# A gated GELU layer on one core: how the first 1024 rows of x and unit 0's weights are loaded, and the order of the opening

## The chip, the core and the metric

The kernel runs on one core of one Trainium2 chip. A core has five engines that run side by side: TensorE (PE) multiplies matrices, with a weight load (PEld) for each product; VectorE (DVE) and ScalarE (ACT) work elementwise and can read and write PSUM, the accumulators of PE; GpSimd (POOL) works elementwise on SBUF alone; SyncE (SP) only issues DMAs here. ScalarE can issue DMAs too. The core's 16 DMA engines serve all queues. The metric is the device time of one execution in microseconds, the median of several runs.

## The reference

```python
def reference(x, w_gate, w_up, w_down):
    g = jnp.einsum("bsd,df->bsf", x, w_gate)
    u = jnp.einsum("bsd,df->bsf", x, w_up)
    h = _gelu(g) * u                       # tanh form
    return jnp.einsum("bsf,fd->bsd", h, w_down)
```

x is 2048 rows of 1024, w_gate and w_up are 1024 x 3584, w_down is 3584 x 1024, all in bf16.

## The kernel before

The 2048 rows are done in two passes (`ip`) of two blocks of 512 rows each (`N = 512`; `c` is 0 or 1). For a product PE needs x with its model dimension on the partitions, so each block is held turned: `xT[c]` is a tile of 128 partitions x 8 x 512, eight slices of k (`NKB = 8`) of 128 each. The 3584 columns of the hidden layer are done in 14 units of 256 columns for gate and up each.

Unit 0 of the first pass is done plainly, in bf16: for each block 32 products of 128 x 128 by 512 (`plain`: eight slices of k for four banks of PSUM, gate and up for two halves of 128 columns), then `finish`: GELU on ACT (`gelu`, L212) and the product of gate and up on DVE (`times`). All later units save products by Strassen-like sums: seven products in place of eight, two of them raw (bf16, straight from x and w, `raw_products`, L227) and five in fp32r from sums that DVE makes of x (`t1` to `t4`, and the cast `tb` on ACT; `sums_t`, L169) and that DVE or POOL makes of the weights (`s1` to `s4`, and the cast `sa` on ACT; `sums_s`, L184). Sums of weights are made on DVE for unit 1 (its s3 on POOL), on POOL for the units after it; POOL is held behind the last t4 by a small copy (`pool_behind`, L199).

The opening, which the change touches, stands at L1038 to L1100:

- SP's queue: four plain loads of block 0's rows (`load_x`, 128 rows of 1024 each, 256 KB), six loads of unit 0's weights `wf` (gate and up in three pieces, k 0 to 1, 2 to 4, 5 to 7; 128, 192 and 192 KB each), unit 1's weights `w` (two loads of 512 KB), four transposing loads of block 1 (`transposing`, two slices of k each, 256 KB), unit 2's weights. A queue issues in this order. DMAs tell of their landing by eight semaphores used in turn, so an issue also waits for the landing of the one that had its semaphore before.
- PE: `NWARM = 7` products of ones into a bank that is overwritten later, then `turn` for each of the four loads of rows: eight transposes by the identity `ident`, which POOL makes, into a PSUM bank, and a copy to `xT[0]` by DVE (by ACT for the second). Two short products of ones stand ahead of the third `turn`. Then block 0's 32 products (the first two slices of k in halves of 256 rows), unit 1's 16 raw products, and, in `rest_of_0(0)` (L1093), block 1's 32 products into banks 4 to 7. Then unit 1's fp32r products: s2 by t2, s1 by t1, s3 by t3, s4 by tb (`unit`, L249), the raw products of units 2 and 3, and sa by t4.
- DVE, from the end of block 0: the two `times` of block 0 with one half of s1 each side of them, s2, s4, t1, t2, the sums of unit 1's raw products (`late`), half of t3, the `times` of block 1, the rest of t3, t4.

The order on SP, DVE, POOL and PE is that of the program; ACT's is too within the opening. Tiles come from pools in which a tile waits until the one that had its place has been read for the last time: the weights' pool has three places.

Of the kernel before, what the change touches and what calls it, by code (L numbers as in the profile page):

```python
# [7 lines left out]


@with_exitstack  # L10
def kernel(
# [23 lines left out]
    nc = tc.nc  # L35
    ENG = mybir.EngineType
    ORDER = {ENG.SP, ENG.DVE, ENG.Pool, ENG.PE}
    P = nc.NUM_PARTITIONS
    bf16 = mybir.dt.bfloat16
# [7 lines left out]
    x2 = x.flatten_outer_dims()  # L47
    out2 = out.flatten_outer_dims()
    S, Dm = x2.shape
    Df = w_gate.shape[1]  # L50

    NKB = Dm // P
    KH = NKB // 2
    NFB = Df // P
    NJ = NFB // 2
    N = 512
    NS = N // P
    NPASS = S // (2 * N)
    NU = NFB // 2
    NWARM = 7  # L60
    SLOTS, SUMS = 36, 13
    FIRST, LAST = 4, 13
    JS = {4: (0, 2), 6: (3, 5), 8: (6, 7), 10: (8, 9), 12: (10, None)}
# [20 lines left out]
    xpool = ctx.enter_context(tc.tile_pool(name="x", bufs=1))  # L84
# [8 lines left out]
    def new_x():  # L93
        return [xpool.tile([P, NKB, N], bf16, name=f"xT{c}") for c in range(2)]
# [11 lines left out]
    def h(kh, j, c):  # L106
        fb = kh * NJ + j
        return hT[:, fb, c, :] if fb < NH else late_h()[:, fb - NH, c, :]
    wdn = w_down.rearrange("(kh j p) d -> p kh j d", kh=2, p=P)

    def slot(shape, dtype, name, sums=False):
        return (spool if sums else kpool).tile(shape, dtype, name=name, tag="s" if sums else "k")
# [5 lines left out]
    bank = [psum.tile([P, N], f32, name=f"bank{i}") for i in range(8)]  # L118
    even, odd, cc, dd = bank[6:8], bank[0:2], bank[2:4], bank[4:6]

    def dve(out, a, b, op):
        nc.vector.tensor_tensor(out=out, in0=a, in1=b, op=op)  # L122
# [22 lines left out]
    def matmul(ps, lhs, rhs, start, stop):  # L145
        nc.tensor.matmul(  # L146
            ps, lhsT=lhs, rhs=rhs, start=start, stop=stop, skip_group_check=True
        )
# [3 lines left out]
    def load_w(u, queue=nc.sync):  # L152
        f0 = u * 2 * P
        w = wpool.tile([P, 2, NKB, 2 * P], bf16, name="w")
        for i, src in enumerate((w_gate, w_up)):
            queue.dma_start(
                out=w[:, i],
                in_=src[:, f0 : f0 + 2 * P].rearrange("(ko ki) f -> ki ko f", ki=P),
            )
        return w  # L160
# [8 lines left out]
    def sums_t(xT):  # L169
        K = range(KH)  # L170
        lo, hi = [[xT[c][:, k] for k in K] for c in range(2)], [
            [xT[c][:, KH + k] for k in K] for c in range(2)
        ]
        return Sums(
            how={
                "t1": lambda q: [new(dve, lo[1][k], lo[0][k], SUB, "t1") for k in K],
                "t2": lambda q: [new(dve, hi[1][k], q["t1"][k], SUB, "t2") for k in K],
                "t3": lambda q, K=K: [new(dve, hi[1][k], lo[1][k], SUB, "t3") for k in K],
                "t4": lambda q: [new(dve, hi[0][k], q["t2"][k], SUB, "t4") for k in K],
                "tb": lambda q: [cast(hi[1][k], "tb") for k in K],  # L180
            }
        )

    def sums_s(w, eng):  # L184
        GU = range(2)
        sh = [P, KH, P]
        a11, a21 = [[w[:, i, :KH, h : h + P] for i in GU] for h in (0, P)]
        a12, a22 = [[w[:, i, KH:, h : h + P] for i in GU] for h in (0, P)]
        return Sums(
            how={  # L190
                "s1": lambda q, GU=GU: [new(eng, a21[i], a22[i], ADD, "s1", sh) for i in GU],
                "s2": lambda q: [new(eng, q["s1"][i], a11[i], SUB, "s2", sh) for i in GU],
                "s3": lambda q: [new(eng, a11[i], a21[i], SUB, "s3", sh) for i in GU],
                "s4": lambda q: [new(eng, a12[i], q["s2"][i], SUB, "s4", sh) for i in GU],
                "sa": lambda q: [cast(a22[i], "sa", sh) for i in GU],
            }
        )
# [14 lines left out]
    def gelu(src):  # L212
        g = slot([P, N], f32, "g")
        nc.scalar.activation(g, src, ACT.Gelu_apprx_tanh)  # L214
        return g
# [3 lines left out]
    def times(fb, c, g, u):  # L219
        at = away[fb, c]() if (fb, c) in away else h(fb // NJ, fb % NJ, c)  # L220
        dve(at, g, u, MUL)
# [5 lines left out]
    def raw_products(e, c, xT, w):  # L227
        for i in range(2):
            product(e[i], w[:, i, :KH, :P], [xT[0][:, k, :] for k in range(KH)], True)
        p1 = [snap(e[i], "p1") for i in range(2)]  # L230
        for i in range(2):
            b21 = [xT[0][:, KH + k, :] for k in range(KH)]
            product(c[i], w[:, i, KH:, :P], b21, True)
        return p1
# [611 lines left out]
    sa = {}  # L846
# [152 lines left out]


    warm = nc.const_aps.tensor(1.0, [P, N], bf16)
    ident = xpool.tile([P, P], bf16, name="ident")
    make_identity(nc, ident)

    def load_x(c):
        t = []
        for i in range(NS):
            xn = slot([P, Dm], bf16, "xn")
            r0 = c * N + i * P
            nc.sync.dma_start(out=xn, in_=x2[r0 : r0 + P, :])  # L1010
            t.append(xn)
        return t

    def turn(xT, xn, c, i):
        tp = bank[4 + i].bitcast(bf16).rearrange("p (k r) -> p k r", k=NKB)
        for ko in range(NKB):
            nc.tensor.transpose(tp[:, ko, :], xn[i][:, ko * P : (ko + 1) * P], ident)
        for ks in (range(NKB),) if i < NS - 1 else (range(KH), range(KH, NKB)):
            ks = slice(ks.start, ks.stop)
            (on_act if i == 1 else on_dve)(out=xT[c][:, ks, i * P : (i + 1) * P], in_=tp[:, ks])  # L1020

    def transposing(xT, c, ko, r0, n=1):
        nc.sync.dma_start_transpose(
            out=xT[c][:, ko : ko + n], in_=x2[r0 : r0 + N, ko * P : (ko + n) * P]
        )

    def load_wf(queue, k0, k1):
        for i, src in enumerate((w_gate, w_up)):
            got = queue.dma_start(
                out=wf[:, i, k0:k1],  # L1030
                in_=src[k0 * P : k1 * P, 0 : 2 * P].rearrange(
                    "(ko ki) f -> ki ko f", ki=P
                ),
            )
            if queue is not nc.sync:
                tc.keep_in_program_order(got)

    xT = new_x()  # L1038
    xn0 = load_x(0)
    wf = wpool.tile([P, 2, NKB, 2 * P], bf16, name="w")  # L1040
    for k0, k1 in ((0, 2), (2, 5), (5, NKB)):
        load_wf(nc.sync, k0, k1)
    w = load_w(1)
    for ko in range(0, NKB, 2):
        transposing(xT, 1, ko, N, 2)
    ahead = load_w(2)

    def plain(ps, c, kos, parts=1):
        n = N // parts
        for k in range(kos.start, kos.stop, 2):  # L1050
            for part in range(parts):
                cols = slice(part * n, (part + 1) * n)
                for p, (j, i) in zip(ps, [(j, i) for j in range(2) for i in range(2)]):
                    for ko in (k, k + 1):
                        matmul(
                            p[:, cols],
                            wf[:, i, ko, j * P : (j + 1) * P],
                            xT[c][:, ko, cols],
                            ko == 0 and part == 0,
                            ko == NKB - 1,  # L1060
                        )

    def finish(ps, c):
        for j in range(2):
            times(j, c, gelu(ps[2 * j]), ps[2 * j + 1])

    on_dve, on_act = nc.vector.tensor_copy, nc.scalar.copy
    s, t = sums_s(w, dve), sums_t(xT)
    with tc.manual_schedule(engines={ENG.Activation}):
        def keep_warm(n, cols):  # L1070
            for _ in range(n):
                nc.tensor.matmul(
                    bank[3][:, :cols], lhsT=warm[:, :P], rhs=warm[:, :cols], start=True, stop=True
                )

        keep_warm(NWARM, N)
        for i in range(NS):
            if i == 2:
                keep_warm(2, 2 * P)
            turn(xT, xn0, 0, i)  # L1080
        plain(bank[0:4], 0, range(0, 2), parts=2)
        plain(bank[0:4], 0, range(2, NKB))
        s["s3"] = sums_s(w, pool)["how"]["s3"](s)
        s["s1"] = s["how"]["s1"](s, range(1))
        finish(bank[0:4], 0)
        s["s1"] += s["how"]["s1"](s, range(1, 2))
        nxt = {"p1": raw_products(odd, cc, xT, w)}
        s.make("sa", "s2", "s4")
        t.make("t1")

    seen = xpool.tile([P, 1], f32, name="seen")

    def rest_of_0(part):  # L1093
        if part == 0:
            plain(bank[4:8], 1, range(NKB))
            t.make("t2", "tb")
        else:
            t3 = t["how"]["t3"](t, range(0, 2))
            finish(bank[4:8], 1)
            t["t3"] = t3 + t["how"]["t3"](t, range(2, KH))  # L1100

    E, K, C, F = odd, cc, dd, even
    S, p5 = {}, {}
# [42 lines left out]
    for ip in range(NPASS):  # L1146
        with tc.manual_schedule(engines={ENG.Activation}):
# [10 lines left out]
            for u in range(1 if ip == 0 else 0, NU):  # L1158
# [113 lines left out]
                s = nxt.pop("s", None)  # L1272
# [35 lines left out]
        if not last:  # L1308
            t, s = got["t"], got["s"]
# [29 lines left out]
```

## Time and profile before

| what | value |
|---|---|
| median of 3 runs | 534.73 us (534.45 to 535.01) |
| the profiled execution | 534.41 us, of which the span of the instructions is 532.6 |
| busy: PE, DVE, ACT, POOL | 526.6, 404.7, 302.1, 268.4 us |
| HBM read, written | 86.38 MB, 31.06 MB |
| the four plain loads of block 0, issue to landing | 3.4 us in the median |
| the four transposing loads of block 1, issue to landing | 4.0 to 6.2 us |

A line of the timeline has the start, the time, the engine, the line, the operation, what it writes and reads, and the count, then the engine's idle time before it and what ended it. PE's products overlap, so a single one's time is longer than its share of the stream: a group's time divided by its count is the better measure. Most of the span is one unbroken stream of products:

```profile
371.51 21.38 PE bank L146 x95
392.89 0.07 issue
392.96 21.39 PE bank L146 x95
```

These lines are from the chain of work that ended last (start, time, what): 0.07 us lie between two stretches of 95 products.

### The profile page before, as it was taken

What the parts mean: (1) busy time and instruction counts of PE and PEld (TensorE: products, weight loads), DVE (VectorE), ACT (ScalarE), POOL (GpSimd) and SP (SyncE); (2) the same over time, 40 slices, a digit from 0 to 9 for tenths busy, and PEclk for the clock granted to TensorE, in tenths of its full rate; (3) what the DMA queues carried; (4) which work ended last, traced back from release to release, by engine and by line L of the source; (5) the groups of instructions that cost most, each with busy time, mean ns of one, the idle gap of its engine ahead of it and who ended that gap; (6) DMA issues with size and microseconds to landing.
All of it is one profiled execution on the core that took longest, in us unless ns stands there. A gap on an engine that the chain in (4) does not pass through costs nothing. (4 is left out here: it accounts for less than half of the span.)

```text
span 532.6 us, 7727 instructions
## 1 busy us (share of the span) xinstructions
PE 526.6 (99%) x2354; PEld 374.6 (70%) x2375; DVE 404.7 (76%) x646; ACT 302.1 (57%) x545; POOL 268.4 (50%) x259
## 2 busy tenths in 40 slices
PE   9999999999999999999999999999999999999997
PEld 5568686867677774588886676767668674588885
DVE  2988768787777786938799977576576679789795
ACT  2557686868585851015546866666656651064471
POOL 1179976979797970000002998695987900000000
PEclk9999999999999999999999999999999999999999
DMA  9966218585767599999899889954472399499994
GB/s 247 247 159 178 79 60 295 198 297 199 236 219 266 183 357 382 380 278 270 224 277 295 256 283 347 321 157 132 107 219 82 129 371 352 163 337 303 233 201 150
DMA packets 140601, 126.09 MB, mean 237 GB/s; under 512 B 31504, under 2 KB 119056, under 8 KB 140432
## 3 DMA queue, kind: packets, MB, share of 16 engines
q1 hardware_dynamic: 136208, 124.55, 77.4%
q10 hardware_dynamic: 4352, 1.05, 1.1%
q8 instruction: 19, 0.31, 0.2%
q14 instruction: 22, 0.18, 0.1%
HBM read 86.38 MB, written 31.06 MB: 221 GB/s over the span
## 5 line engine op out<-in xcount | busy, mean ns | idle before, releaser
L125 POOL TENSOR_TENSOR s<-w 128x512 fp32r<-128x512 bf16 x102 | 117.5, 1170 | 48.7 <-DMA w<-in_w_gate_dram 33.0
L146 PE MATMUL bank<-t,s 128*128 128x512 f32 x528 | 126.3, 392 | 0.0
L146 PEld LDWEIGHTS bank<-t,s 128*128 128x128 f32 x528 | 99.0, 188 | 21.6 <-POOL s L125 0.3
L146 PE MATMUL bank<-xT,w 128*128 128x512 bf16 (+1 forms) x489 | 107.8, 376 | 1.3 <-DMA w<-in_w_up_dram 0.3
L146 PEld LDWEIGHTS <-w 128*128 128x128 bf16 x504 | 47.9, 98 | 58.6 <-issue 3.9
L214 ACT ACTIVATE g<-sum 128x512 f32<-128x512 f32 x81 | 51.5, 636 | 59.4 <-DVE sum L122 58.6
L139 ACT COPY p<-bank 128x512 f32<-128x512 f32 x98 | 55.2, 590 | 46.5 <-PE bank L146 46.3
L122 DVE TENSOR_TENSOR hT<-g,bank 128x512 bf16<-128x512 f32 x72 | 49.0, 687 | 17.5 <-ACT g L214 11.3
L125 POOL TENSOR_TENSOR s<-w,s 128x512 fp32r<-128x512 bf16 x50 | 57.8, 1175 | 0.4
L125 POOL TENSOR_TENSOR s<-s,w 128x512 fp32r<-128x512 f32 x50 | 57.4, 1165 | 0.3
L146 PE MATMUL bank<-q 128*128 128x512 f32 x224 | 56.3, 391 | 0.0
L122 DVE TENSOR_TENSOR bank<-bank,p 128x512 f32<-128x512 f32 x74 | 51.3, 695 | 5.8 <-PE bank L146 5.3
L146 PE MATMUL bank<-t,sa 128*128 128x512 f32 x216 | 54.9, 397 | 0.0
L200 POOL COPY seen<-t 128x1 f32<-128x1 f32 x2 | 0.4, 183 | 107.4 <-DVE t L122 107.4
L146 PE MATMUL bank<-tb,s 128*128 128x512 f32 x216 | 54.3, 393 | 0.0
L146 PEld LDWEIGHTS bank<-q 128*128 128x128 f32 x224 | 42.0, 188 | 9.3 <-DMA q<-td 0.4
L146 PEld LDWEIGHTS bank<-t,sa 128*128 128x128 f32 x216 | 40.6, 188 | 9.1
L146 PEld LDWEIGHTS bank<-tb,s 128*128 128x128 f32 x216 | 40.5, 188 | 9.0 <-POOL s L125 0.3
L122 DVE TENSOR_TENSOR sum<-bank,p 128x512 f32<-128x512 f32 x54 | 37.0, 686 | 12.7 <-PE bank L146 11.3
L139 ACT COPY u<-bank 128x512 f32<-128x512 f32 x62 | 35.5, 596 | 17.7 <-PE bank L146 14.1
L134 ACT CAST tb<-raw 128x512 fp32r<-128x512 bf16 x20 | 11.9, 635 | 38.3 <-DMA raw<-in_w_down_dram 32.0
L134 ACT CAST sa<-w 128x512 fp32r<-128x512 bf16 x54 | 30.7, 617 | 3.7 <-DMA out_dram<-st 3.7
(123 smaller groups left out, 733.4 us busy)
## 6 DMA issues: line engine op xcount, KB each, us to landing
raw<-in_w_down_dram SPq DMA_DIRECT2D x72, 256.0 KB, 5.7
w<-in_w_gate_dram SPq DMA_DIRECT2D x27, 512.0 KB, 4.6
w<-in_w_up_dram SPq DMA_DIRECT2D x27, 512.0 KB, 6.2
td<-m SPq DMA_DIRECT2D x11, 768.0 KB, 5.1
q<-td SPq DMA_DIRECT2D x28, 256.0 KB, 5.5
pd<-xT SPq DMA_DIRECT2D x10, 512.0 KB, 5.8
w<-td SPq DMA_DIRECT2D x5, 1024.0 KB, 9.3
p<-pd SPq DMA_DIRECT2D x20, 256.0 KB, 5.1
```

What stands on the lines that cost most here:

```text
L122: nc.vector.tensor_tensor(out=out, in0=a, in1=b, op=op)
L125: nc.gpsimd.tensor_tensor(out=out, in0=a, in1=b, op=op)
L134: nc.scalar.copy(out=t, in_=src)
L139: nc.scalar.copy(out=t, in_=ps)
L146: nc.tensor.matmul(ps, lhsT=lhs, rhs=rhs, start=start, stop=stop, skip_group_check=True)
L200: nc.gpsimd.tensor_copy(out=seen, in_=tile[:, :1].bitcast(f32))
L214: nc.scalar.activation(g, src, ACT.Gelu_apprx_tanh)
```

## The change

Block 0 is no longer loaded as rows and turned on PE, but by four transposing loads on SP's queue, at its very start, as block 1 is; block 1's four follow at once, ahead of unit 1's weights. Unit 0's weights are issued on ScalarE's queue. The identity, the 32 transposes and the copies out of PSUM are gone, the two short products of ones too; there are eight long ones in place of seven. Block 0's products are no longer split by halves. Block 1's products stand right behind block 0's, ahead of unit 1's raw ones. On DVE the order is: the `times` of block 0, t1, t2, s1, s2, the `times` of block 1, half of t3, the sums of unit 1's raw products, the rest of t3, s4, t4. What comes behind is unchanged.

```diff
@@ -4,7 +4,6 @@
 import concourse.tile as tile
 from concourse import bass_utils, mybir
 from concourse._compat import with_exitstack
-from concourse.masks import make_identity
 
 
 @with_exitstack
@@ -57,7 +56,7 @@
     NS = N // P
     NPASS = S // (2 * N)
     NU = NFB // 2
-    NWARM = 7
+    NWARM = 8
     SLOTS, SUMS = 36, 13
     FIRST, LAST = 4, 13
     JS = {4: (0, 2), 6: (3, 5), 8: (6, 7), 10: (8, 9), 12: (10, None)}
@@ -999,25 +998,6 @@
 
 
     warm = nc.const_aps.tensor(1.0, [P, N], bf16)
-    ident = xpool.tile([P, P], bf16, name="ident")
-    make_identity(nc, ident)
-
-    def load_x(c):
-        t = []
-        for i in range(NS):
-            xn = slot([P, Dm], bf16, "xn")
-            r0 = c * N + i * P
-            nc.sync.dma_start(out=xn, in_=x2[r0 : r0 + P, :])
-            t.append(xn)
-        return t
-
-    def turn(xT, xn, c, i):
-        tp = bank[4 + i].bitcast(bf16).rearrange("p (k r) -> p k r", k=NKB)
-        for ko in range(NKB):
-            nc.tensor.transpose(tp[:, ko, :], xn[i][:, ko * P : (ko + 1) * P], ident)
-        for ks in (range(NKB),) if i < NS - 1 else (range(KH), range(KH, NKB)):
-            ks = slice(ks.start, ks.stop)
-            (on_act if i == 1 else on_dve)(out=xT[c][:, ks, i * P : (i + 1) * P], in_=tp[:, ks])
 
     def transposing(xT, c, ko, r0, n=1):
         nc.sync.dma_start_transpose(
@@ -1036,68 +1016,52 @@
                 tc.keep_in_program_order(got)
 
     xT = new_x()
-    xn0 = load_x(0)
     wf = wpool.tile([P, 2, NKB, 2 * P], bf16, name="w")
     for k0, k1 in ((0, 2), (2, 5), (5, NKB)):
-        load_wf(nc.sync, k0, k1)
-    w = load_w(1)
+        load_wf(nc.scalar, k0, k1)
+    for ko in range(0, NKB, 2):
+        transposing(xT, 0, ko, 0, 2)
     for ko in range(0, NKB, 2):
         transposing(xT, 1, ko, N, 2)
+    w = load_w(1)
     ahead = load_w(2)
 
-    def plain(ps, c, kos, parts=1):
-        n = N // parts
-        for k in range(kos.start, kos.stop, 2):
-            for part in range(parts):
-                cols = slice(part * n, (part + 1) * n)
-                for p, (j, i) in zip(ps, [(j, i) for j in range(2) for i in range(2)]):
-                    for ko in (k, k + 1):
-                        matmul(
-                            p[:, cols],
-                            wf[:, i, ko, j * P : (j + 1) * P],
-                            xT[c][:, ko, cols],
-                            ko == 0 and part == 0,
-                            ko == NKB - 1,
-                        )
+    def plain(ps, c):
+        for k in range(0, NKB, 2):
+            for p, (j, i) in zip(ps, [(j, i) for j in range(2) for i in range(2)]):
+                for ko in (k, k + 1):
+                    matmul(
+                        p, wf[:, i, ko, j * P : (j + 1) * P], xT[c][:, ko],
+                        ko == 0, ko == NKB - 1,
+                    )
 
     def finish(ps, c):
+        g = [gelu(ps[2 * j]) for j in range(2)]
         for j in range(2):
-            times(j, c, gelu(ps[2 * j]), ps[2 * j + 1])
-
-    on_dve, on_act = nc.vector.tensor_copy, nc.scalar.copy
+            times(j, c, g[j], ps[2 * j + 1])
+
     s, t = sums_s(w, dve), sums_t(xT)
     with tc.manual_schedule(engines={ENG.Activation}):
-        def keep_warm(n, cols):
-            for _ in range(n):
-                nc.tensor.matmul(
-                    bank[3][:, :cols], lhsT=warm[:, :P], rhs=warm[:, :cols], start=True, stop=True
-                )
-
-        keep_warm(NWARM, N)
-        for i in range(NS):
-            if i == 2:
-                keep_warm(2, 2 * P)
-            turn(xT, xn0, 0, i)
-        plain(bank[0:4], 0, range(0, 2), parts=2)
-        plain(bank[0:4], 0, range(2, NKB))
+        for _ in range(NWARM):
+            matmul(bank[3], warm[:, :P], warm, True, True)
+        plain(bank[0:4], 0)
+        finish(bank[0:4], 0)
+        t.make("t1")
+        plain(bank[4:8], 1)
+        t.make("t2", "tb")
         s["s3"] = sums_s(w, pool)["how"]["s3"](s)
-        s["s1"] = s["how"]["s1"](s, range(1))
-        finish(bank[0:4], 0)
-        s["s1"] += s["how"]["s1"](s, range(1, 2))
+        s.make("sa", "s1", "s2")
+        finish(bank[4:8], 1)
         nxt = {"p1": raw_products(odd, cc, xT, w)}
-        s.make("sa", "s2", "s4")
-        t.make("t1")
 
     seen = xpool.tile([P, 1], f32, name="seen")
 
     def rest_of_0(part):
         if part == 0:
-            plain(bank[4:8], 1, range(NKB))
-            t.make("t2", "tb")
+            t["t3"] = t["how"]["t3"](t, range(0, 2))
         else:
-            t3 = t["how"]["t3"](t, range(0, 2))
-            finish(bank[4:8], 1)
-            t["t3"] = t3 + t["how"]["t3"](t, range(2, KH))
+            t["t3"] += t["how"]["t3"](t, range(2, KH))
+            s.make("s4")
 
     E, K, C, F = odd, cc, dd, even
     S, p5 = {}, {}
```

## The prediction

> **What bounds the kernel now.** I read the page first, then PE's waits, then the first 25 us in order of time, then the DMA queues.
>
> ```profile
> span 532.6 us, 7727 instructions
> PE 526.6 (99%) x2354; PEld 374.6 (70%) x2375; DVE 404.7 (76%) x646; ACT 302.1 (57%) x545; POOL 268.4 (50%) x259
> PE bank L1072 <- PEq L1323: 0.8, 1, 0.8
> PE bank L146 <- DMA w<-in_w_up_dram: 0.3, 1, 0.3
> ```
>
> The last two lines are all that PE waits for in the whole span: 0.8 us for the start, 0.3 us for one piece of unit 0's weights. PE is the bound throughout; what the opening saves or loses on PE goes into the total one for one, unless a later wait takes it back.
>
> ```profile
> 0.77 3.14 PE L1072 MATMUL bank<-const-bfloat16-1.0 128*128 128x512 bf16 x7 [0.77 <-PEq L1323]
> 3.71 1.91 PE L1017 MATMUL bank<-ident,xn 128*128 128x128 bf16 x16
> 5.42 0.44 PE L1072 MATMUL bank<-const-bfloat16-1.0 128*128 128x256 bf16 x2
> 5.70 1.08 PE L1017 MATMUL bank<-ident,xn 128*128 128x128 bf16 x16
> 6.72 0.38 PE L146 MATMUL bank<-xT,w 128*128 128x256 bf16 x2
> 9.83 7.50 PE L146 MATMUL bank<-xT,w 128*128 128x512 bf16 x34
> 24.32 5.84 PE L146 MATMUL bank<-t,s 128*128 128x512 f32 x24
> ```
>
> Columns: start, time, line, operands, count. The opening is seven idle-filling matmuls, 32 transposes of x, then 80 bf16 products (32 of block 0, 16 raw ones of unit 1, 32 of block 1), and at 24.32 unit 1's first fp32 product. One full product takes (7.50 - 0.38) / 33 = 0.216 us. PE runs at half rate at first: (3.71 - 0.77) / 7 = 0.42 us per filler, and the first 16 transposes take 1.91 us, the next 16 only 1.08. The granted-clock row shows nothing of this (9 in every slice).
>
> **The mark.** 48 products (10.4 us) lie between the end of unit 0's block 0 and unit 1. The record at 24.32 stands 0.2 us ahead of its predecessor's end, so that block ends at 24.5 - 10.4 = 14.15 us. The change swaps the order of those 48 but not their number; the forecast is where this 14.15 goes.
>
> **What it takes away.** 32 transposes and two short fillers (3.71 to 6.72, 3.0 us of PE), the 0.3 us wait, five copies out of PSUM (DVE 2.0 us, ACT 1.0) and POOL's identity. One filler comes on (0.43): PE is free at 0.77 + 8 x 0.427 = 4.2 us, 2.5 earlier. If data lay ready, 32 products, three of them at half rate before 5.5, would end at 11.7: a ceiling of 2.4 us of gain. Data will not lie ready.
>
> **What it adds: four transposing loads at the very start, beside six weight loads on another queue.** Transposing loads stand in the trace, and so does that mixture:
>
> ```profile
> 8.23 7.74 SPq L1023 DMA_TRANSPOSE xT<-in_x_dram  x4
> xT<-in_x_dram SPq DMA_TRANSPOSE x1, 2.5
> 10.00:11.00 1.00, 1.00 (x6) 0.48 (x5) 0.00 (x0) 0.00 (x0) 0.00 (x0) 1.00 1.21 295
> 13.40:14.60 1.20, 1.20 (x8) 0.51 (x6) 0.74 (x2) 0.85 (x2) 1.06 (x2) 1.00 1.28 288
> 498.50:502.50 4.00, 4.00 (x20) 3.30 (x19) 4.00 (x8) 2.27 (x5) 0.00 (x0) 1.00 1.17 193
> DMA packets 2953, 1.35 MB, mean 225 GB/s; under 512 B 2125, under 2 KB 2953, under 8 KB 2953
> q1 hardware_dynamic: 892, 0.85, 63.4%
> q10 hardware_dynamic: 2061, 0.50, 51.9%
> ```
>
> Last column of the window rows: GB/s. Weight loads alone move 295, transposing loads alone 288. The last three lines are the window 497 to 503, where ScalarE's queue (q10) holds transposing loads and SP's (q1) copies: together 225, in its middle 193, the transposing loads 0.50 MB / 6 us = 83, the copies 0.85 / 6 = 142. The new opening is this mixture with the queues exchanged.
>
> A transposing load of 256 KB (0.262 MB) keeps SP's queue 1.30 us where nothing is ahead of it (the last two of L1023), and its data start when the issue ends. The lone one (128 KB, at 256 us, landing 2.5 after issue) gives the tail: 2.5 - 1.13 of issue - 0.131 / 288 (0.46) = 0.9 us from last byte to landing.
>
> Taking the nearest row, 83 GB/s for x and for the weights 142 x 295 / 355 = 118, some 120 (their packets are 512 bytes, the row's 1 KB; 355 is the best of the 40 slices of that window):
> - x pieces (two of eight k each): the first issued 0.74 to 2.04, data to 5.2, landed 6.1; the second 9.3. From 10.7, when the weights are through, 288: third 11.9, fourth 12.8.
> - weights, 1.05 MB from 2.0 (x's first loads now move 53 GB/s before that): the six pieces land at 4.0, 5.1, 6.7, 8.4, 10.0, 11.6. The sixth issue waits on ScalarE for the first x piece (eight DMA semaphores in turn), 6.1, before its turn comes at 9.1: no loss. Behind it stand only a table load and the first GELU, not due before 14.
> - PE: first pair of k (8 products) from 6.1 to 7.8 at full rate, 9.5 at half; second from 9.5 at the latest to 11.2; third waits to 11.9, ends 13.6; fourth 15.3.
>
> So block 0 ends at 15.3, not 14.15: **+1.15 us**. Between full and half rate in the first pair the sum is the same, since the second piece covers it.
>
> The bounds. Below: both queues together at 295, half each. Then the x pieces land at 4.75, 6.5, 8.3, 10.1, the last weight piece at 10.0, and block 0 ends at 12.8: -1.35. Above: packets served in turn, 256 bytes of x for 512 of weights, at the 193 of the window's middle: x at 64, landing at 7.05, 11.1, 12.0, 13.0; block 0 ends at 16.3: +2.15. I take 83 because that row holds this very pair of kinds on this pair of queues.
>
> On the second queue itself the Trainium skill, DMA: Bandwidth & Descriptors, section "Issuing engines are not separate DMA queues", says that loads issued from several engines run on the same 16 engines, and a second issuer saves issue time alone. The 225 in the mixture against 295 and 288 alone agrees and is worse. By that rule without the loss, the sum would be the lower bound, -1.35.
>
> **What is moved.** Block 1's four loads now stand behind block 0's on SP: the second waits for x's second piece (9.3), so their issues end at 13.2 or so and, with data from 11.9 at 288, they land at 13.7 to 16.5; block 1's products run from 15.3, 1.73 us a pair: no wait. Unit 1's weights follow on SP, issued from 13.2; before, they took 6.1 and 7.4 us to land: 19.3 and 21.1 against need at 15.3 + 6.9 = 22.2. Unit 2's weights land some 4 us later; POOL first reads them after t4, at 30. Unit 3's wait for the end of block 1's products, then load_lo's transposes, first read at 40.35, landed before at 30.5.
>
> On DVE s1 and s2 come behind t1 and t2, and s4 ahead of t4. From block 0's last hT to t4 it now does 26 operations in place of 25: t4 is 0.62 us later against PE. Hidden: unit 2's raw products reach the first bank that DVE must free at 33.8 (32.04 plus eight products), DVE is done with it at 32.7. Without that cover it costs up to 0.6. s2 is done 8.7 us after the end of block 0, needed 10.4 after; s4 14.4 against 16.2. POOL starts later by the same 0.6, and has 5.4 us in hand (unit 2's s2 ends at 34.99, read at 40.35).
>
> **Sum.** 534.41 (profiled execution; span 532.6) + 1.15 = 535.6; that execution stands 0.3 below the median 534.73, so **535.9** against the median.
>
> **Rivals.**
> 1. *The queues share without loss*: block 0 ends at 12.8, -1.35, 533.4. For it: 497 to 498.5 in the same mixture moves close to 300. Against: the middle of that window, 193. Chance 0.25.
> 2. *The clock stays at half.* PE stands idle from 4.2 to about 6, and again between pieces. Half rate to 12.3 with the x pieces of the upper bound: second pair 11.1 to 13.4, third 15.2, fourth 16.9: +2.75, 537.5. It decides once the first pieces land after 5.5, when the rate now doubles. Against: most of the stretch to 9.5 is busy. The Trainium skill, TensorE: Matmul & The Clock Gate, Part 1, has the gate open after about 3.4 us of sustained activity and close after an idle window as long; the trace agrees that some 4.7 us of work come before the doubling. Chance 0.13.
> 3. *SP's queue is the bound.* Eight transposing loads at the 7.74 / 4 = 1.93 us of L1023 hold it to 16.2; unit 1's weights land at 22.3 and 24.1 (6.1 and 7.4 after). With block 0 at 12.8, the raw up products then wait to 24.1 and end at 26.7: +2.2, 536.9. Against: the 1.93 holds a wait for a full ring. Chance 0.1.
> 4. *Gain and loss cancel* (PE's 2.5 us against a mixture half as bad): 534.7. Chance 0.07.
>
> **From cases to numbers.** The forecast has 0.45. 0.2% (1.07 us) is about what a measurement of this kernel can tell from no change. Faster: rival 1 less its smaller half, 0.22. Slower: forecast 0.31, rivals 2 and 3 0.23, together 0.54. Same: 0.24. Range: 533.2 (rival 1) to 537.8 (rival 2); the forecast's own, 535.2 to 537.0.
>
> **What would show it.** x's first piece landing near 6 and the second near 9, PE idle ahead of products of L145 on DMA xT<-in_x_dram, some 2 us between 4.2 and 6.1 and 0.5 or more later; unit 1's first fp32 product near 25.5, in place of 24.3; everything after it shifted by the same. First piece before 5 and no later waits: rival 1. Products 0.43 apart beyond 9: rival 2. PE waiting for w after block 1: rival 3. A fp32 product after 25 waiting for DVE would make the hidden 0.62 wrong.

## The result: slower by some 2.5 us, lost in the first 45 us

| | before | after |
|---|---|---|
| median (runs) | 534.67 us (6) | 536.7 us (6; 536.34 to 538.44) |
| ratio to before, 95% interval | | 1.0047 (1.0031 to 1.0063) |
| profiled execution, its span | 534.41, 532.6 | 538.44, 536.7 |
| a second trace of the kernel after, its span | | 536.86, 535.0 |

The first trace of the kernel after is of the slowest of its six runs, so a second one was taken; it lies near the median of the six (two more runs taken with it took 538.9 and 539.67). Most readings below give both.

The page of the first trace of the kernel after:

```profile
span 536.7 us, 7653 instructions
PE 528.2 (98%) x2334; PEld 371.7 (69%) x2334; DVE 404.1 (75%) x642; ACT 299.5 (56%) x543; POOL 268.0 (50%) x257
```

and the waits of PE and of its weight loads (PEld) that the text uses (for what, us in total, times, longest):

```profile
PE bank L145 <- DMA xT<-in_x_dram: 3.0, 2, 2.6
PE bank L145 <- DVE hT L121: 1.0, 1, 1.0
PE bank L145 <- PEq L1287: 0.8, 1, 0.8
PEld bank L145 <- DVE t L121: 0.7, 2, 0.4
```

PE itself waited 1.1 us in the whole span before, 4.8 now. Two of its three waits are new, and they are of two kinds: 3.0 us for x, 1.0 us for VectorE. PE's busy time has risen too (526.6 to 528.2) though 32 transposes are gone: some of its work ran slower. The opening in order of time (start, time, what, count, idle before), first trace:

```profile
0.78 3.57 PE L145 MATMUL bank<-const-bfloat16-1.0 128*128 128x512 bf16 x8 [0.78 <-PEq L1287]
4.72 2.55 PE L145 MATMUL bank<-xT,w 128*128 128x512 bf16 x8 [0.37 <-DMA xT<-in_x_dram]
9.86 17.20 PE L145 MATMUL bank<-xT,w 128*128 128x512 bf16 x72 [2.59 <-DMA xT<-in_x_dram]
26.70 6.33 PE L145 MATMUL bank<-t,s 128*128 128x512 f32 x24
32.87 2.00 PE L145 MATMUL bank<-tb,s 128*128 128x512 f32 x8
37.61 5.34 PE L145 MATMUL bank<-xT,w 128*128 128x512 bf16 x24 [1.00 <-DVE hT L121]
42.60 2.19 PE L145 MATMUL bank<-t,sa 128*128 128x512 f32 x8
```

and in the second:

```profile
5.28 3.57 PE L145 MATMUL bank<-xT,w 128*128 128x512 bf16 x8 [0.94 <-DMA xT<-in_x_dram]
9.71 15.70 PE L145 MATMUL bank<-xT,w 128*128 128x512 bf16 x71 [0.85 <-DMA xT<-in_x_dram]
25.06 6.34 PE L145 MATMUL bank<-t,s 128*128 128x512 f32 x24
31.24 1.98 PE L145 MATMUL bank<-tb,s 128*128 128x512 f32 x8
35.97 5.34 PE L145 MATMUL bank<-xT,w 128*128 128x512 bf16 x24 [1.02 <-DVE hT L121]
40.96 1.28 PE L145 MATMUL bank<-t,sa 128*128 128x512 f32 x4
```

and the line of the kernel before with which the last ones are compared:

```profile
38.55 2.19 PE L146 MATMUL bank<-t,sa 128*128 128x512 f32 x8
```

Two points of these lists are marks, since the same products stand ahead of them in all kernels here but for a few in the opening: unit 1's first fp32 product (24.32 before) and its first product of t4 with the cast sa, called t x sa below (38.55 before). In the first trace they are 2.38 and 4.05 us late, in the second 0.74 and 2.41. So each trace loses a part ahead of the first mark, which differs (the loads), and 1.67 us between the marks, the same in both. After t x sa nothing changes: the spans differ from before's by 4.1 and 2.4.

Where the 1.6 us between the two traces lie, the granted clock tells. Windows of the first trace (stretch, its length, busy time of PE, PEld, DVE, ACT, POOL, then the clock, the DMA share, GB/s):

```profile
8.00:10.00 2.00, 0.14 (x1) 0.10 (x1) 0.00 (x0) 0.00 (x0) 0.00 (x0) 0.88 1.26 172
10.00:12.00 2.00, 2.00 (x6) 0.64 (x5) 0.00 (x0) 0.00 (x0) 0.00 (x0) 0.50 1.25 291
12.00:14.00 2.00, 2.00 (x9) 0.83 (x8) 0.00 (x0) 0.00 (x0) 0.00 (x0) 0.77 1.10 227
```

and of the second:

```profile
10.00:12.00 2.00, 2.00 (x11) 0.90 (x10) 0.00 (x0) 0.00 (x0) 0.00 (x0) 1.00 1.27 260
```

PE was busy all of 10 to 12 in both, with 6 products in the first and 11 in the second. In the first the clock had risen at 6.1, and fell to half again at 9.5, after the 2.59 us without work, until 12.9. In the second it rose only at 9.25, when the half-rate products of the first pair were done and covered by the wait for the second piece.

### The profile page after: what moved, and what is told of

It reads as the page before. It is cut to its first block, busy times and chain, and to the rows that moved or that the text cites. A ratio compares the mean times of both kernels' runs of the same rounds, so it can differ in the third digit from the quotient of the medians.

```text
span 536.7 us, 7653 instructions
## 1 busy us (share of the span) xinstructions
PE 528.2 (98%) x2334; PEld 371.7 (69%) x2334; DVE 404.1 (75%) x642; ACT 299.5 (56%) x543; POOL 268.0 (50%) x257
## 4 chain that ended last, share of the span: by engine, by line
PE 94%; DVE 3%; DMA 1%; issue 1%; SPq 0%; ACT 0%; DVEq 0%
PE bank L145 94%; DVE t L121 2%; DMA xT<-in_x_dram 1%; DVE hT L121 0%; DVE s L121 0%; SPq L1003 0%; DVE bank L121 0%; DVE sum L121 0%; ACT g L213 0%; DVE st L859 0%; ACT st L858 0%; DVEq L121 0%
## 5 line engine op out<-in xcount | busy, mean ns | idle before, releaser
L145 PE MATMUL bank<-xT,w 128*128 128x512 bf16 x496 | 112.6, 385 | 4.0 <-DMA xT<-in_x_dram 3.0
L121 DVE TENSOR_TENSOR sum<-bank,p 128x512 f32<-128x512 f32 x54 | 37.0, 685 | 12.8 <-PE bank L145 10.5
L138 ACT COPY u<-bank 128x512 f32<-128x512 f32 x62 | 35.4, 596 | 18.7 <-PE bank L145 15.4
```

Source lines behind the costliest of these rows:

```text
L138: nc.scalar.copy(out=t, in_=ps)
L145: nc.tensor.matmul(ps, lhsT=lhs, rhs=rhs, start=start, stop=stop, skip_group_check=True)
```

## The experiments

The distance to before at t x sa and in the span (us) is from one trace of each kernel (before: 38.55 and 532.6); the ratio is from all runs, each against the kernel before on its own chip (medians 534.16 to 534.67). The last column has the time of the traced execution and the median of all runs: where the two differ by 1 us or more, the distances of that row are not typical.

| kernel | t x sa | span | ratio (interval) | traced, median |
|---|---|---|---|---|
| loads alone, 8 fillers | 0.0 | +0.5 | 1.0025 (1.0013 to 1.0037) | 534.92, 536.12 |
| loads alone, one queue | +1.2 | +1.1 | 1.0025 (1.0014 to 1.0037) | 535.61, 535.86 |
| loads alone, 11 fillers, two traces | +0.2, +0.5 | +2.5, +1.4 | 1.0036 (1.0021 to 1.0051), 1.0040 (1.0024 to 1.0056) | 536.86, 535.90; 535.80, 536.23 |
| the same, raw products regrouped | +0.9 | +1.5 | 1.0039 (1.0025 to 1.0052) | 535.85, 536.14 |
| order alone | +1.7 | +2.0 | 1.0034 (1.0022 to 1.0046) | 536.40, 536.41 |
| order alone, s3 early | -0.3 | -0.3 | 0.9998 (0.9990 to 1.0007) | 534.13, 534.22 |
| after, s3 early | +0.3 | +1.2 | 1.0049 (1.0030 to 1.0067) | 535.64, 536.43 |
| after, one queue | +3.5 | +4.6 | 1.0060 (1.0045 to 1.0075) | 539.03, 537.91 |
| after, 12 more fillers | +4.4 | +5.2 | 1.0062 (1.0042 to 1.0082) | 539.59, 537.67 |
| only the weights on ScalarE's queue | +5.6 | +5.8 | 1.0083 (1.0067 to 1.0098) | 540.19, 539.08 |
| after, second trace | +2.4 | +2.4 | 1.0074 (1.0049 to 1.0099), 3 runs | 536.86, 538.90 (of all nine runs of after: 536.87) |

**The two halves of the change.** The loads alone: the kernel before, with block 0 by four transposing loads, the weights on ScalarE's queue and eight fillers; order and VectorE's work as before.

```
-    xn0 = load_x(0)
     ...
     for k0, k1 in ((0, 2), (2, 5), (5, NKB)):
-        load_wf(nc.sync, k0, k1)
+        load_wf(nc.scalar, k0, k1)
+    for ko in range(0, NKB, 2):
+        transposing(xT, 0, ko, 0, 2)
     w = load_w(1)
     ...
-        for i in range(NS):
-            if i == 2:
-                keep_warm(2, 2 * P)
-            turn(xT, xn0, 0, i)
-        plain(bank[0:4], 0, range(0, 2), parts=2)
-        plain(bank[0:4], 0, range(2, NKB))
+        plain(bank[0:4], 0, range(NKB))
```

> Block 0 by four transposing loads at the head of SP's queue and unit 0's weights on ScalarE's queue, as in the change; everything else (unit 1's weights ahead of block 1's loads, its raw products ahead of block 1's, DVE's order) as before. Theory A (the loads are late in the mixture of two queues, PE idles for x's second piece, its clock may fall to half): that piece lands near 9.8 and block 0 ends at 15.0 (full rate) to 16.5 (half), against 14.15: ratio 1.0015 to 1.0045. Rival B (the loads cost nothing, the new order does it): block 0 ends at 12.8 or earlier and the time is below before, ratio 0.997 to 0.999.

Theory A's ratio came (1.0025), but not its signs: in the trace, which is of one of the fastest runs, x's second piece landed at 8.18. Block 0 ended at some 13.4 (24 products of 0.216 from 8.22), 0.7 ahead of before, and PE then waited for unit 1's up weights, which landed at 14.99 (13.61 before):

```profile
8.22 6.20 PE L146 MATMUL bank<-xT,w 128*128 128x512 bf16 x28 [0.94 <-DMA xT<-in_x_dram]
15.04 9.67 PE L146 MATMUL bank<-xT,w 128*128 128x512 bf16 x44 [0.61 <-DMA w<-in_w_up_dram]
```

So this execution loses nothing up to t x sa, and what the typical run loses isn't shown by it.

The order alone: the kernel before, with block 1's loads ahead of unit 1's weights, block 1's products ahead of the raw ones, and VectorE's order of the kernel after; x by plain loads and transposes.

```
+    for ko in range(0, NKB, 2):
+        transposing(xT, 1, ko, N, 2)
     w = load_w(1)
-    for ko in range(0, NKB, 2):
-        transposing(xT, 1, ko, N, 2)
     ...
         finish(bank[0:4], 0)
+        t.make("t1")
+        plain(bank[4:8], 1, range(NKB))
+        t.make("t2", "tb")
+        s["s3"] = sums_s(w, pool)["how"]["s3"](s)
+        s.make("sa", "s1", "s2")
+        finish(bank[4:8], 1)
+        nxt = {"p1": raw_products(odd, cc, xT, w)}
```

> Block 0's rows and unit 0's weights as before; only the order is changed: block 1's loads ahead of unit 1's weights, block 1's products ahead of unit 1's raw ones, DVE's order with s1, s2 behind t1, t2 and s4 ahead of t4. Theory A with what the trace of after added (two of DVE's t2 sums took 1.64 us in place of 0.68 beside POOL's s3, and PE waited 1.0 us for hT and 0.7 for t3): block 0 still ends at 14.2, and at most 0.5 to 1.7 us are lost behind it: ratio 1.000 to 1.003. Rival B: the whole loss, ratio 1.0035 to 1.005.

Each half costs by itself: 1.0025 and 1.0034 (the second lies between the ranges of its two theories; the 1.7 us at t x sa are the upper end of theory A's). Together they make 1.0059, inside both intervals of the whole change. The order alone has the same 1.7 us between the marks as the kernel after, with an untouched opening (first fp32 product at 24.35), so that part isn't the loads'. VectorE and GpSimd in the kernel with the order alone, in order of time:

```profile
17.59 4.41 DVE L122 TENSOR_TENSOR t<-xT,t 128x512 fp32r<-128x512 bf16 x4
18.04 1.24 POOL L125 TENSOR_TENSOR s<-w 128x512 fp32r<-128x512 bf16 x1 [16.74 <-DMA w<-in_w_gate_dram]
19.82 1.63 POOL L125 TENSOR_TENSOR s<-w 128x512 fp32r<-128x512 bf16 x1 [0.53 <-DMA w<-in_w_up_dram]
```

The four t2 sums took 4.41 us, as in the first trace of the kernel after. In the kernel before they take 2.49, and GpSimd's two s3 differences stand elsewhere:

```profile
11.89 2.94 POOL L125 TENSOR_TENSOR s<-w 128x512 fp32r<-128x512 bf16 x2 [10.59 <-DMA w<-in_w_gate_dram]
20.57 2.49 DVE L122 TENSOR_TENSOR t<-xT,t 128x512 fp32r<-128x512 bf16 x4
```

The two slow ones of the order alone (18.19 and 20.36, 1.64 us each; the others 0.68) are those that stand beside GpSimd's s3; the first ends at 19.83, which is 0.55 after GpSimd's 18.04 + 1.24 = 19.28, and the second at 22.00, again 0.55 after GpSimd's 21.45: each seems to do its work only when GpSimd is done. But unit 1's weights were landing just then (17.97 and 19.75), so the landing could be blamed as well.

**What holds VectorE.** Two kernels let GpSimd make its two s3 differences from unit 0's weights, so that they run 10 to 15 us earlier: the same instructions, at another time. Unit 1's rows that come from s3 are not the reference's.

```
-        s["s3"] = sums_s(w, pool)["how"]["s3"](s)
+        s["s3"] = sums_s(wf, pool)["how"]["s3"](s)
```

In the order alone:

> The kernel before with the new order alone, and GpSimd's two s3 differences read from unit 0's weights, so that they run at about 12 us and not at 18.0 and 19.8; unit 1's rows that come from s3 are then not the reference's. Theory A: the t2 sums fall from 1.64 to 0.68 us, the waits for t3 and hT go, t x sa starts within 0.3 us of before's 38.55 (the order alone had 40.26), ratio 0.9995 to 1.001. Theory B: the sums stay, ratio 1.0025 to 1.0045. Theory C: the sums fall, yet TensorE still waits for VectorE, as t4 is one operation later than before: ratio 1.001 to 1.002.

```profile
7.91 2.26 POOL L125 TENSOR_TENSOR s<-w 128x512 fp32r<-128x512 bf16 x2 [6.61 <-DMA w<-in_w_gate_dram]
17.25 2.49 DVE L122 TENSOR_TENSOR t<-xT,t 128x512 fp32r<-128x512 bf16 x4
```

(VectorE and GpSimd of that kernel in order of time.) The sums are back at 2.49 us, PE waits for nothing but the start, t x sa stands at 38.23, and the whole loss is gone: 0.9998. Theory A holds; the landing (B) is out, since unit 1's weights still land while the t2 sums run (17.46 and 19.23); and so is C, since one operation more ahead of t4 costs nothing once the collision is away. On this the Trainium skill, SBUF — State Buffer, section "Who interferes with whom", has a rule: a VectorE instruction with both inputs in SBUF and a GpSimd instruction that reads SBUF exclude each other, and the one that comes second is blocked until the first is done. The 0.68 us that became 1.64 beside 1.24 us of GpSimd, and only there, agree with it.

In the kernel after:

> The kernel after, with GpSimd's two s3 differences of unit 1 read from unit 0's weights (landed at 11.3 us) in place of unit 1's (landed at 20.7 and 22.5): the same two instructions on the same engine, some 9 us earlier; unit 1's rows that come from s3 are then not the reference's. Theory A (the two t2 sums of 1.64 us in place of 0.68 were held by GpSimd's s3): both t2 sums fall to 0.6-0.7, t4 ends 1.9 us earlier behind the end of block 0, TensorE's waits for t3 (0.6) and hT (1.0) go, and the time falls by 1.5 us from the kernel after: a ratio to before of 1.001 to 1.003. Theory B (they were held by the landing of unit 1's weights in SBUF): both stay at 1.6 us and the ratio stays at 1.0035 to 1.006. Theory C (the lateness on VectorE is real but costs nothing at the end): the sums fall and the ratio stays.

Half a miss. For the sums theory A holds: t2 takes 2.49 us. But the wait for hT did not go. t x sa is only 0.27 behind before, but the first mark is 0.51 ahead of before's (23.81; x's second piece landed at 7.98 in this execution), so between the marks 0.78 of the 1.67 us are still lost: VectorE now stood idle for 0.93 us until unit 1's up weights landed at 21.05, and PE waited 0.63 us for hT. In time theory A does not hold: 1.0049, where 1.001 to 1.003 was expected; 1.0 us of the span's distance came behind t x sa, most of it in the middle (below). The six runs spread over 3.3 us, so a gain of 1 us may hide in them, but none is shown.

**Does the second queue cost?** All six weight pieces back on SP, between x's pieces, first in the kernel after:

```
-    for k0, k1 in ((0, 2), (2, 5), (5, NKB)):
-        load_wf(nc.scalar, k0, k1)
-    for ko in range(0, NKB, 2):
+    for ko, k in zip(range(0, NKB, 2), ((0, 2), (2, 5), (5, NKB), None)):
+        if k:
+            load_wf(nc.sync, *k)
         transposing(xT, 0, ko, 0, 2)
```

> After, with unit 0's weights on SP's queue too, each pair of pieces ahead of the piece of x that it goes with. Theory A (two queues hold each other up): x's first piece lands near 4.8, the second near 7, the fourth near 10.5, block 0 ends at 12.4 to 13 and the time is 1.5 to 3.5 us below after, ratio to before 0.998 to 1.001. Rival C (transposing loads are slow beside weight loads on any queue, or so early): the second piece still lands near 9 or later and the ratio stays at 1.003 to 1.006.

Then, with the same edit, in the loads alone:

> The transposing loads alone (order, products and VectorE as before, 8 fillers) with unit 0's weights issued by SP between them. Theory T: ratio 1.0025 to 1.0045, as with the loads and ScalarE's queue. Theory Q: ratio 0.999 to 1.0015.

Neither is faster than its partner with two queues: 1.0060 against 1.0047, and 1.0025 against 1.0025. Theory A of the first run is out (x's second piece landed at 8.39 there, a little earlier than rival C had it, and the ratio is C's), and theory Q of the second nearly so: its upper end, 1.0015, is the lower end of the interval. In the loads alone the x pieces land at 5.01, 8.18, 10.63 and 11.79 from one queue and at 5.36, 8.18, 9.56 and 11.02 from two. What is left is the mixture of transposing loads with copies, whoever issues them. That one queue or two make no difference but for the issue is what the Trainium skill says in DMA: Bandwidth & Descriptors, section "Issuing engines are not separate DMA queues"; that the mixture is slow is this case's own finding. The DMA view of the kernel after from 2 to 11 us, which is where the weights and x come in:

```profile
DMA packets 5712, 1.93 MB, mean 214 GB/s; under 512 B 3694, under 2 KB 5712, under 8 KB 5712
q1 hardware_dynamic: 3598, 0.90, 63.9%
q10 hardware_dynamic: 2114, 1.03, 54.9%
```

and the same stretch of the kernel before, with plain loads of x on one queue:

```profile
DMA packets 3980, 2.72 MB, mean 302 GB/s; under 512 B 175, under 2 KB 3481, under 8 KB 3980
```

The last test of the second queue gives it to the kernel before, and leaves x to plain loads:

```
     for k0, k1 in ((0, 2), (2, 5), (5, NKB)):
-        load_wf(nc.sync, k0, k1)
+        load_wf(nc.scalar, k0, k1)
```

> The kernel before with unit 0's six weight pieces from ScalarE's queue and nothing else changed: x comes by plain loads and is turned by TensorE. The three kernels with the loads alone were 1.5 to 1.9 us slower in the median, though in their profiled runs the start was at most 0.9 us behind before's. Theory T (the transposing loads are what costs): ratio 0.999 to 1.001. Theory Q (weights from a second queue cost, whatever x does): ratio 1.0025 to 1.004.

Neither theory had 1.0083. SP's four plain loads of x and PE's transposes in that kernel:

```profile
0.74 3.77 SPq L1010 DMA_DIRECT2D xn<-in_x_dram  x4
6.07 0.62 PE L1017 MATMUL bank<-ident,xn 128*128 128x128 bf16 x8 [0.21 <-DMA xn<-in_x_dram]
9.47 1.04 PE L1017 MATMUL bank<-ident,xn 128*128 128x128 bf16 x8 [2.77 <-DMA xn<-in_x_dram]
```

The four issues took 1.82 us before and take 3.77 here. Ten transfers now start at once on eight completion semaphores, and x's fourth load is the one that had to wait for the first weight piece to land (4.16); it landed at 9.42 in place of 6.11, behind all the weights. PE stood for 2.77 us and the clock fell to half from 8.6 to 15.4. The run says what a wrong place in that turn costs; its time doesn't settle T against Q, which the pair with the loads alone does. Its transfers do speak for T: from 2 to 11 us plain loads from two queues moved as much as from one.

```profile
DMA packets 4228, 2.83 MB, mean 314 GB/s; under 512 B 175, under 2 KB 3739, under 8 KB 4228
```

**The clock.** Twelve more fillers in the kernel after, between the first and the second pair of k, were to keep the clock up:

```
         for k in range(0, NKB, 2):
+            if c == 0 and k == 2:
+                for _ in range(12):
+                    matmul(bank[4], warm[:, :P], warm, True, True)
```

> After, with twelve filler products (2.6 us at full rate) between block 0's first and second pair of k, so that PE is not idle while x's second piece is late; the loads are the same. If the half rate from 9.5 to 12.9 in the trace of after is the cost of that idle time: the products from 9.9 run at 0.216 each, block 0 ends at 15.0 and the ratio falls by 0.001 to 0.003 against after (1.0047), in the runs in which the clock fell. If the late pieces alone do it: the same as after.

No gain is shown: 1.0062 against 1.0047, with intervals that overlap. The traced run, the slowest of the six, can't test the idea, since the clock was still low when the fillers began (it rose at 9.46): they took 3.0 us in place of 2.6, and the second pair, whose x had landed at 8.72, started at 11.70. In the loads alone, three more fillers at the start:

> The transposing loads alone with 11 fillers in place of 8, so that TensorE has work from 0.8 to about 5.5 us, past the landing of the first piece (4.7 to 5.4). Theory A (the spread of the loads alone, 534.6 to 536.9, comes from the phase of the clock gate: some of its windows hold so much idle time that the clock stays at half): the gate opens before 7.6 us in every run, unit 1's first fp32 product starts at 24.2 to 24.6, runs within 0.8 us of each other, ratio 0.9993 to 1.001. Theory D (the spread comes from the loads themselves): same spread as with 8, ratio 1.0015 to 1.004.

As expected the clock rose at 6.08 and stayed up, and the first fp32 product came at 24.45. But the runs still spread, from 534.49 to 539.1, and the slowest had a mean granted clock of 1.000 (a fall for 3.41 us would take 0.003 off it), so theory A of the spread falls. The trace shows where 2.3 of its 2.5 us went: not in the opening.

```profile
PE bank L146 <- DMA q<-td: 1.0, 1, 1.0
PE bank L146 <- DMA raw<-in_w_down_dram: 0.8, 1, 0.8
```

(PE's waits in the kernel with the loads alone and 11 fillers.) They stand at 245 and 209 us, in a stretch where SP issues one transfer after another. A second trace of that kernel:

> The transposing loads alone with 11 fillers, for a second trace: the first was 0.2 us behind before at 40 us and 2.3 us behind at 270 us, after waits of 0.81 us for a piece of w_down (at 209 us) and 1.01 us for q (at 245 us). Theory M (those waits come from the execution and not from the kernel): they are absent or elsewhere, and the distance between 150 and 300 us changes by less than 1 us. Theory K (the kernel's other transfers make them): they stand at the same places, each over 0.5 us.

```profile
PE bank L146 <- DMA xT<-in_x_dram: 1.6, 1, 1.6
PE bank L146 <- DMA raw<-in_w_down_dram: 0.7, 1, 0.7
```

The wait for w_down is there again at 209 us, as K has it; the one for q is not, and between 150 and 300 us the distance grew by 0.6 us where it had grown by 2.1, as M has it (behind t x sa in all: 0.9 and 2.3). That is between M and K. x's second piece landed at 9.41 here and at 8.29 in the first trace, without any change of the kernel.

With the raw products of unit 1 in the order gate, gate, up, up:

```
-        nxt = {"p1": raw_products(odd, cc, xT, w)}
+        for i in range(2):
+            product(odd[i], w[:, i, :KH, :P], [xT[0][:, k, :] for k in range(KH)], True)
+            product(cc[i], w[:, i, KH:, :P], [xT[0][:, KH + k, :] for k in range(KH)], True)
+        nxt = {"p1": [snap(odd[i], "p1") for i in range(2)]}
```

> The same with unit 1's raw products in the order gate, gate, up, up in place of gate, up, gate, up, so that the half of unit 1's weights that lands last (15.0 us) is asked for after 8 products and not after 4. In the loads alone TensorE waited 0.61 us for it. Theory A: that wait goes and nothing takes its place, 0.4 to 0.7 us below the 11-filler run: ratio 0.998 to 0.9995. Rival: another wait (ScalarE's copies of the raw products, or VectorE's t2) takes the time back: ratio as the 11-filler run's.

The 0.61-us wait for the up weights went, as expected, but x's second piece landed at 9.44 and PE waited 1.95 us for it; the ratio is the other's (1.0039 and 1.0036). No version here beats the kernel before.

**The second trace of the kernel after.**

> The kernel after as it is, for a second trace: its first was of the slowest of six runs (538.44; the median was 536.7) and stood 4.05 us behind before at the end of the start (40 us). If the start decides the run's time, t x sa starts at 40.3 to 41.0 us (1.7 to 2.4 behind before's 38.55) in a run near the median, and the distance stays the same up to the end. If something in the middle decides it, the distance at 40 us is another than at the end by over 0.5 us.

t x sa at 40.96 and the same 2.4 us in the span: in both traces of the kernel after the start decides the time, and the middle adds nothing. Of its nine runs in both rounds only two (538.44, the first trace, and 539.67) had a mean granted clock of 0.995; the others had 0.998 to 1.000. So the fall of the clock that cost the first trace 1.6 us is the rarer case. Two runs were nearly as slow without it (537.77 and 538.9); of these there is no trace.

## Why the prediction came out as it did, step by step

The forecast was +1.2 us and "slower"; measured are +2.0 between the medians and +2.5 by the ratio. The direction and its first reason (the mixture of transposing loads and copies) held; the size was short by a term that the sum had at nothing.

For the step that failed, these are the lines of t4 before (first) and in the first trace after (last), and of t2 in that trace (start, time):

```profile
27.78 2.49 DVE L122 TENSOR_TENSOR t<-xT,t 128x512 fp32r<-128x512 bf16 x4
19.94 4.41 DVE L121 TENSOR_TENSOR t<-xT,t 128x512 fp32r<-128x512 bf16 x4
32.69 2.48 DVE L121 TENSOR_TENSOR t<-xT,t 128x512 fp32r<-128x512 bf16 x4
```

- *PE is the bound, and what the opening loses goes into the total.* Held for the kernel after: the distance at t x sa is the distance of the spans, in both traces.
- *The ceiling, PE free at 4.2.* Held: the fillers end at 4.35.
- *The mixture.* Held in its total rate and at the second piece, which decides; the first piece came some 1 us earlier than forecast, which gained nothing, as PE then waited for the second. The pieces were to land at 6.1, 9.3, 11.9 and 12.8 and landed at 4.68, 9.82, 11.56, 12.23 in the first trace and 5.24, 9.67, 10.55, 12.27 in the second; the last weights at 11.32 and 11.51 for 11.6. The stretch from 2 to 11 moved 214 GB/s, for which the sum had 203. Block 0 was to end at 15.3. By the first fp32 product, with the 0.2 and 10.4 us of the prediction's mark, it ended at 16.5 and at 14.9: +2.4 and +0.7 for the +1.15. The row at 497 us was the right one to take.
- *Half rate in the first pair alone, hidden by the second piece.* Held in the second trace, failed in the first: there the low clock lay on the second pair and the third, where nothing covers it. That is the mechanism of rival 2, in one of two traces and at 2.4 us for its 2.75. The Trainium skill's rule that the prediction cited, TensorE: Matmul & The Clock Gate, Part 1, has the clock fall after about 3.4 us without work; here it fell after 2.59, while 1.95 us of waiting (the kernel with regrouped raw products) left it up; the trace decides.
- *Rival 1, the queues share without loss.* Out: x's second piece lands at 9.7 and not at 6.5. *Rival 3, SP's queue as the bound.* Out: the eight issues end at 14.9, not at 16.2, and PE never waits for w. *Unit 1's weights* land at 20.7 and 22.5, or 20.1 and 21.9, some 1 us later than the 19.3 and 21.1 forecast.
- *t4 is 0.62 us later and hidden.* This is the step that failed. Against the end of block 0 (the marks above), t4 ended at +16.1 us before (30.27) and at +18.6 in the first trace after (35.17): 2.5 later, 0.6 by the operation more and 1.9 by two sums that GpSimd blocked. The 0.62 by itself is hidden as forecast (the order alone with s3 early loses nothing); what the sum left out is that VectorE's sums themselves grow longer. The cover of the prediction, DVE done 1.1 us ahead of PE, is less than that, and PE waits 1.0 us for the hT product (which frees a bank) and, in its weight loads, 0.7 for t. In the second trace t2's last sum starts just ahead of GpSimd (20.10 against 20.13) and isn't held; VectorE waits 0.50 us for unit 1's up weights there, and then one sum of s1 and one of s2 are held (s1's 1.06 us in place of 0.68, s2's pair 2.24 in place of 1.28), with the same 1.67 us as the result. VectorE's durations were taken from a trace in which GpSimd worked at 11.9 to 14.8, while VectorE did little; the change moved both onto each other. The test that the prediction named, an fp32 product after 25 that waits for VectorE, came out against it in the weight loads' 0.7 us; the longer wait, for hT, is a bf16 product's.

The change thus costs in two places, the loads (1.0025 alone) and the order (1.0034 alone, of which the early s3 gives everything back; in the kernel after it gives back about half of the 1.67 us between the marks). Open is the last part of the loads' cost: in the kernels with the loads alone, the traces show 0 to 1.2 us at t x sa, while the ratios say 1.3 to 2.1 us. The trace with 0.0 is of a run 1.2 us faster than its median, which may be a part of it. Another part is lost between 150 and 300 us, in waits for transfers among other things (0.6 and 2.1 us in the two traces with 11 fillers); it differs between executions of one kernel, the kernel before has one trace alone, and why these kernels lose more there was not found. Whether the kernel after would gain from s3 on another engine was not tried.

## What to carry to other kernels

When work is moved in time, take each operation's duration together with what the neighbouring engine does at its new place: a sum that takes 0.68 us in the old trace took 1.64 beside GpSimd. Price a transposing load from a row in which copies run beside it, not from a row where it runs alone. And where an opening waits in pieces, look at which pieces the low clock falls on: the same 3.4 us cost nothing under one wait and 1.6 us behind it.

## What the runs showed of the hardware

- Transposing loads and copies together moved 208 and 230 GB/s from 2 to 11 us on one queue (two traces) and 214 to 247 on two (eight traces); plain loads moved 302 on one queue and 314 on two.
- A VectorE sum with both inputs in SBUF that started while a GpSimd difference ran ended 0.54 to 0.55 us after that (six sums in three traces), and took up to 1.64 us in place of 0.68.
- The clock rose or fell only at steps of 3.41 us: at 6.09, 9.51 and 12.92 in the first trace of the kernel after, at 5.16, 8.57 and, two steps on, 15.40 with the weights alone on ScalarE's queue. The phase of the steps differed between executions (4.2 to 6.5 us for the first rise in most kernels, 9.3 to 10.0 in three). By the idle time of PE that fell inside one such step: 0.94 us kept the clock from rising (4.34 to 5.28, second trace of the kernel after; the rise came a step later, at 9.25), 0.37 did not (4.35 to 4.72, the first), nor 0.55 (4.35 to the rise at 4.90, the loads alone with 8 fillers). Once up, 1.75 left it up (7.54 to the end of the step at 9.29, the regrouped raw products); 2.1 (within 5.16 to 8.57, weights on ScalarE's queue alone) and 2.2 (7.27 to 9.51, the first trace) brought it down.
- The ten transfers that start the kernel share eight completion semaphores over both queues: a load in the wrong place waits for a stranger's landing (x's fourth load, 3.3 us late).
